# One-pass contraction in the early weighted sums of an attention + SwiGLU kernel, with pair 0's preparation and the weight conversions planned anew

## The chip, the cores and the metric

The kernel runs on one core of a Trainium2 chip. The metric is the device time of one execution in microseconds (us), the median of several runs. The core has five instruction streams that concern us: PE (TensorE, matmuls), DVE (VectorE), ACT (ScalarE), POOL (GpSimd) and SP (SyncE, which here only issues DMAs). They run side by side and wait for each other through semaphores.

## The reference, cut to what matters

```python
q, k, v: (8, 12, 448, 64)          # batch, heads, sequence, head_dim, float32
q_n = q / sqrt(mean(q*q, -1) + 1e-6) * g_q          # the same for k with g_k
attn = softmax(q_n @ k_n.T / 8)                     # over the 448 keys
x = (attn @ v), heads side by side: (3584, 768)
g, val = x @ w_gate, x @ w_val                      # (768, 1536) each, stored as float64
out = (g * sigmoid(g) * val) @ w_out                # (1536, 768), stored as float64
```

## The kernel before, in words

**Tiling.** Two heads of one batch make a pair; there are 48 pairs, six for each batch. A pair holds its two heads one above the other in the 128 partitions (64 of head_dim each). Two batches make one of four blocks of the feed-forward part (896 tokens). The feed-forward part computes its products by a fast 3x3 scheme with 15 products in place of 18: sums of blocks of the operands (function `sides` for the tokens, `convert` for the weights) are multiplied, and the results are added up in PSUM and SBUF ("reads").

**Stages.** First come the 12 early pairs (`m < EARLY`, both batches of block 0), alone on PE. Then block 0's up products (120 products of two matmuls each, gate products into `mm` banks and value products into `at` banks, line 1416), then its down products (line 1594) with pairs 12 to 23 between them, then block 1, and so on. Only the early stage and block 0 also carry the conversion of the weights: 24 pieces are loaded (L1215, L1217), turned from float64 to float32 on ACT (L1225, L1229) and DVE (L1246, L1252, L1258), combined on POOL (L1279, L1282: 15 results) and stored to DRAM (L1307), from where the up and down products load them (L1371).

**A pair.** `attention(m)` does: load q, k (L748 for the early pairs) and v (L771, L774); square q and k on ACT (L784); add up each head's squares on DVE (L804); the inverse root, estimated on ACT (L698, L699) and improved on DVE (L704 to L706); scale on POOL (L843); eight transposes on PE (L869, `turn`); copy the turned k to SBUF on DVE (L875) and the turned q on ACT with the gains `gg` (L877). Then scores in four pieces of keys j = 3, 0, 1, 2 (L927; j = 3 is half a piece), with an exp on ACT after each (L942); the weighted sums (L1003, `weighted`) over the four pieces; the sums of the exps (L1034, `total`); the inverse of these (DVE L1070 and L1072, ACT L1085 `exchange`, DVE L1089 `spread`); and the division (L1098).

**The weighted sums before.** For each key piece of 128 rows, four matmuls work on quarters of the array: 64 keys by 64 values each, 448 queries long. So the upper and the lower 64 keys land in two banks (`at` 0 and 1), which ACT copies out (L1092, `copy_sums`) and DVE joins (L1095, `join`).

**What sets the order.** The order of instructions on each engine is written by a planner, the class `Order`: each piece is added with an engine, a duration, a due time (`when`), what it comes `after`, and the buffers that it takes and uses; `run` then imitates the engines with those durations and emits each piece where its imitation starts it. `LEAD`, `PAIR`, `FIRST`, `MORE`, `block_start` and `pair_time` set the due times, `rank` a lead over others, `SWITCH` a price for a change of mode. On the chip each engine follows its own emitted order, and waits only for semaphores. Buffers matter too: two pairs of `st` banks for scores and for turned q and k, two `at` banks, seven `e` tiles, and nine places for conversions (two in `xs`, `hs`, `spare`, three in `gt`, `es`, and the pairs' `work`), which the stages of the kernel share.

Of the kernel before, what the change touches and what calls it, by code (L numbers as in the profile page):

```python
# [364 lines left out]
class Order:  # L365
# [10 lines left out]
    SWITCH = dict(PE=0.1, ACT=1.3)  # L376
    HOP, ISSUE, LANDING, PLACES = 0.15, 0.54, 2.0, 8

# [52 lines left out]
    def run(self, lookahead=400):  # L431
# [3 lines left out]
        while any(left.values()):  # L435
            best = None
            for engine, pieces in left.items():
                choice = None
                last = self.last.get(engine, dict(group=None))
                for piece in pieces[:lookahead]:  # L440
# [10 lines left out]
                    if choice is None or at < choice[0] - 0.4:  # L451
                        choice = (at, piece)
# [40 lines left out]
def fast(  # L493
# [62 lines left out]
    R = S // NJ  # L556

# [26 lines left out]
    def take(name, key, shape):  # L584
        if name in ("e", "ea"):
            at = order.turn[name] % BUFS[name]
            tiles[name, key] = es[:, at] if at < BUFS["e"] else more_es[:, at - BUFS["e"]]
            return tiles[name, key]
        if name in OFTEN:
# [21 lines left out]
        pool = psum if name in ("st", "at") else sbuf  # L611
# [31 lines left out]
    banks = [psum.tile([P, TB], F32, name=f"mm{i}", bufs=1) for i in range(2)]  # L643
    many = const.tile([P, C], F32, name="many")
# [10 lines left out]
    LEAD, PAIR = 10.6, 8.97  # L655
# [4 lines left out]
    MORE = 6.4  # L660
# [29 lines left out]
    def inverse_root(m, sums, of, when, rank=0.0, tiny=0.0):  # L690
# [10 lines left out]
        def improve():  # L701
# [4 lines left out]
            times(rr, ss, 1.5, rr, op0=ALU.add, op1=ALU.mult)  # L706

# [15 lines left out]
    def attention(m):  # L723
# [52 lines left out]
        load_v = add("SP", 2.4, ready - 16.0, load_values, takes=[("v", m)], moves=VALUE_MOVES, early=25.0)  # L776

        def square(x):
# [5 lines left out]
            nc.scalar.activation(tiles["t", m][:, x], of, AF.Square)  # L784
            if m == 0 and x == 0:
                for _ in range(3):
                    nc.tensor.matmul(banks[0], ident[0:R], of, start=True, stop=True)

        squares = []
        for x in range(2):  # L790
            squares.append(
                add(
                    "ACT", 0.63 if natural else 0.58, ready - 18.0, lambda x=x: square(x),
# [4 lines left out]


# [21 lines left out]
        def both():  # L821
# [5 lines left out]
        sums = add(  # L827
            "DVE", 1.45 if natural else 1.08, ready - 17.0, summed, after=squares, uses=[("t", m)], takes=[("ss", m)]
# [10 lines left out]
        def scale(x):  # L839
            if natural:  # L840
                split = dict(h=2, j=NJ, d=D)
                rr = tiles["rr", m][:, ts(x, 2 * NJ)].rearrange("p (h j one) -> p h j one", h=2, one=1)
                nc.gpsimd.tensor_tensor(  # L843
# [13 lines left out]
                "POOL", 0.98, ready - 9.0, lambda x=x: scale(x), after=[rr], port=True,  # L857
# [6 lines left out]
        def turn(x):  # L864
# [3 lines left out]
            for j in range(NJ):  # L868
                nc.tensor.transpose(turned[:, ts(j, R)], tiles["t", m][:, x, ts(j, P)], ident[0:R, 0:R])  # L869

# [19 lines left out]
        if natural:  # L890
            of_turned = ("st", (m, "turned"))
            for x in (1, 0):
                qt = add(
                    "PE", 0.4, ready - 6.0, lambda x=x: turn(x), after=[scaled[1 - x], qt],
                    uses=[("t", m)] + [of_turned] * (1 - x), takes=[of_turned] * x, mode="full",
                )
                kt = kt or qt
# [7 lines left out]
            )  # L905
        kt = kt or add(
# [89 lines left out]
        def weighted(j):  # L996
            for x in range(2):
                if j == 0:
                    take("at", (m, x), [P, TB])
                rows = ds(D * x, D)  # L1000
                queries = ds(0, S) if j < NJ - 1 else ts(x, Q)
                for h in range(2):
                    nc.tensor.matmul(  # L1003
                        tiles["at", (m, x)][ds(D * h, D), queries],
                        tiles["v", m][rows, j, h],
                        tiles["e", (m, j)][rows, h],
# [37 lines left out]
        last = None  # L1044
        for j in range(NJ):
# [6 lines left out]
                group=("c", m + 1), mode="quarters",  # L1052
            )
        clusters[m, "weighted"] = last
        den = ("st", (m, "d"))
        all_sums = clusters[m, "total"] = add(
            "PE", 1.5 if early else 0.38, when + (0.05 if early else 0.3), total,
            after=[last, *adds] + ([bank_read[0]] if of_bank else []),
            uses=[weights_of(j) for j in range(NJ)] if early else [("sums", m)],
            takes=[] if of_bank else [den], group=("c", m + 1), mode="strips",  # L1060
        )
        if m == EARLY - 1:
            last_exp[0] = all_sums
# [11 lines left out]
        def inverse():  # L1075
            if not early:
                return tiles["at", (m, 0)][:, 0:S]
            return bank[:, 0:S] if of_bank else spread_st[0][:, 1, 0:S]

# [708 lines left out]
```

## Time and profile before

| what | us |
|---|---|
| median of 3 runs | 1462.22 (1462.16 to 1463.76) |
| the profiled execution's own time | 1464.89 |
| its span in the profile | 1463.1 |
| PE busy | 1429.7 (98%) |
| DVE busy | 881.6 (60%) |
| ACT busy | 605.4 (41%) |
| POOL busy | 398.3 (27%) |
| first score matmul of pair 0 (L927) | 14.85 |
| first sum matmul of pairs 0, 1, 2 (L1034) | 34.76, 43.66, 52.52 |
| first up product of block 0 (L1416) | 134.66 |
| last up product of block 0 starts | 313.65 |
| first score matmul of pair 12 | 318.02 |

The profile is of one execution, and times in it count from the span's start. "Busy" counts an engine's instructions; a stretch of PE can be busy at half clock. In the timeline, a line is a run of like instructions: start, length, engine, source line, what is written from what, the shape, the count, and in brackets how long the engine had been idle before it and what ended that. Most matmuls leave two records (those of L869 one), so "x16" of L927 is eight matmuls.

### The profile page before, as it was taken

The numbers are of one execution on the slowest core, as the hardware profiler recorded it, in microseconds if no ns is written. First come the engines' busy times: TensorE is split into PE (matmuls) and PEld (weight loads), VectorE is DVE, ScalarE is ACT, GpSimd is POOL, SyncE is SP. The second block draws the span as 40 slices with busy tenths as digits, with TensorE's granted clock in tenths as the row PEclk, the third lists the DMA queues.
The fourth block names the chain that finished last, engine by engine and source line by source line (L and its number), as shares of the span: only waits on it lengthen the run. The fifth ranks groups of instructions, "written<-read, shape, count | busy, mean of one in ns | idle before, by whom it ended". The sixth has DMA issues, their size and how long they took to land.

```text
span 1463.1 us, 19387 instructions
## 1 busy us (share of the span) xinstructions
PE 1429.7 (98%) x6726; PEld 685.1 (47%) x6726; DVE 881.6 (60%) x1493; ACT 605.4 (41%) x1222; POOL 398.3 (27%) x471
## 2 busy tenths in 40 slices
PE   6998999999999999999999999999999999999997
PEld 2443555544444455544444455554444445555553
DVE  3889977867866444446767632365676643432533
ACT  5885543457563221355654222254656322122100
POOL 3555786535343000012434200012344300000000
PEclk9999999999999999999999999999999999999999
DMA  7667998954454523443553532453454452322235
GB/s 209 185 189 254 337 313 285 297 139 92 102 103 96 133 72 109 110 101 87 118 116 71 118 99 75 117 118 84 103 116 87 96 134 73 102 78 81 78 99 108
DMA packets 410415, 193.28 MB, mean 132 GB/s; under 512 B 280004, under 2 KB 390852, under 8 KB 410308
## 3 DMA queue, kind: packets, MB, share of 16 engines
q1 hardware_dynamic: 399040, 190.57, 48.3%
q10 hardware_dynamic: 11140, 1.38, 0.7%
q8 instruction: 55, 0.90, 0.3%
q14 instruction: 52, 0.43, 0.1%
q0 software_dynamic: 128, 0.00, 0.0%
HBM read 157.29 MB, written 34.60 MB: 131 GB/s over the span
## 4 chain that ended last, share of the span: by engine, by line
PE 90%; DVE 3%; ACT 2%; DMA 2%; issue 1%; SPq 1%; POOL 0%; DVEq 0%; ACTq 0%; POOLq 0%
PE mm L1416 25%; PE at L1416 25%; PE mm L1594 23%; PE st L927 8%; PE at L1003 7%; PE st L1034 1%; ACT es L942 1%; PE mm L1034 1%; DMA out_dram<-spare 1%; DMA work<-in_k_dram 1%; DVE xs L1132 0%; PE st L869 0%; DMA xs<-in_moe_w_gate_dram 0%; DVE spare L1642 0%; DVE mm L1252 0%
## 5 line engine op out<-in xcount | busy, mean ns | idle before, releaser
L1416 PE MATMUL mm<-xs,ws 128*128 128x448 f32 x960 | 400.3, 540 | 0.0
L1416 PE MATMUL at<-xs,ws 128*128 128x448 f32 x960 | 400.2, 539 | 0.0
L1416 PEld LDWEIGHTS at<-xs,ws 128*128 128x128 f32 x960 | 182.3, 190 | 178.9 <-issue 174.7
L1416 PEld LDWEIGHTS mm<-xs,ws 128*128 128x128 f32 x960 | 182.4, 190 | 178.8 <-issue 174.1
L850 POOL TENSOR_TENSOR work<-work,rr 128x448 f32<-128x448 f32 x72 | 67.0, 952 | 468.6 <-DVE rr L706 381.9
L1594 PE MATMUL mm<-gt,ws 128*128 128x448 f32 x448 | 176.1, 544 | 0.0
L927 PE MATMUL st<-work 64*64 64x448 f32 (+1 forms) x1536 | 157.6, 517 | 13.7 <-ACT es L942 6.2
L942 ACT ACTIVATE es<-st 128x896 f32<-128x896 f32 x129 | 114.1, 913 | 110.5 <-PE at L1003 94.1
L1594 PE MATMUL mm<-hs,ws 128*128 128x448 f32 x384 | 151.8, 546 | 0.0
L1354 DVE TENSOR_TENSOR gt<-gt,mm 128x448 f32<-128x448 f32 x64 | 39.8, 621 | 184.3 <-PE mm L1416 182.8
L947 POOL TENSOR_TENSOR sums<-es 128x896 f32<-128x896 f32 x36 | 77.5, 2153 | 184.2 <-PE st L1034 111.2
L1594 PEld LDWEIGHTS mm<-gt,ws 128*128 128x128 f32 x448 | 83.5, 190 | 83.2 <-issue 81.7
L1490 ACT ACTIVATE st<-gt 128x448 f32<-128x448 f32 x96 | 52.6, 547 | 164.9 <-DVE gt L1358 82.0
L1352 ACT COPY gt<-mm 128x448 f32<-128x448 f32 x80 | 42.5, 531 | 167.4 <-PE mm L1416 167.2
L1003 PE MATMUL at<-es,v 64*64 64x448 f32 x1032 | 109.0, 538 | 2.6 <-DVE xs L1095 2.6
L1594 PEld LDWEIGHTS mm<-hs,ws 128*128 128x128 f32 x384 | 71.5, 191 | 72.9 <-issue 71.8
L927 PEld LDWEIGHTS st<-work 64*64 64x64 f32 x1536 | 51.9, 136 | 86.8 <-issue 40.1
L1352 ACT COPY v<-at 128x448 f32<-128x448 f32 x96 | 50.9, 530 | 76.4 <-PE at L1416 74.0
L947 POOL TENSOR_TENSOR sums<-sums,es 128x896 f32<-128x896 f32 x36 | 75.2, 2089 | 2.8
L1003 PEld LDWEIGHTS at<-es,v 64*64 64x64 f32 x1032 | 40.1, 134 | 61.5 <-issue 54.5
L784 ACT ACTIVATE work<-work 128x448 f32<-128x448 f32 (+1 forms) x96 | 55.2, 587 | 25.8 <-DMA work<-in_q_dram 17.1
L1354 DVE TENSOR_TENSOR v<-v,at 128x448 f32<-128x448 f32 x64 | 39.7, 621 | 41.2 <-PE at L1416 41.2
(160 smaller groups left out, 1566.9 us busy)
## 6 DMA issues: line engine op xcount, KB each, us to landing
ws<-up_sides SPq DMA_DIRECT2D x32, 1024.0 KB, 5.6
ws<-down_sides SPq DMA_DIRECT2D x16, 1024.0 KB, 5.7
ws<-down_sides SPq DMA_DIRECT2D x28, 512.0 KB, 4.6
ws<-up_sides SPq DMA_DIRECT2D x16, 768.0 KB, 4.8
out_dram<-spare SPq DMA_DIRECT2D x168, 56.0 KB, 2.1
v<-in_v_dram SPq DMA_DIRECT2D x96, 96.0 KB, 2.6
ws<-up_sides SPq DMA_DIRECT2D x32, 256.0 KB, 5.9
ws<-up_sides SPq DMA_DIRECT2D x16, 512.0 KB, 5.8
```

Of the source, the lines that this page charges most:

```text
L784: nc.scalar.activation(tiles["t", m][:, x], of, AF.Square)
L850: nc.gpsimd.tensor_tensor(out=tiles["t", m][:, x], in0=tiles["qk", (m, x)], in1=rr.to_broadcast([P, NC, C]), op=ALU.mult,)
L927: nc.tensor.matmul(st[ds(D * x, D), h, 0:n], tiles["KT", m][rows, ds(P * j + D * of_keys, D)], tiles["QT", m][rows, ds(Q * of_queries, n)] ...
L942: nc.scalar.activation(e, tiles["st", (m, j)][:, :, 0 : S * width(j) // P], AF.Exp)
L947: nc.gpsimd.tensor_tensor(out=to, in0=tiles["e", (m, 0)] if j == 1 else to, in1=e, op=ALU.add)
L1003: nc.tensor.matmul(tiles["at", (m, x)][ds(D * h, D), queries], tiles["v", m][rows, j, h], tiles["e", (m, j)][rows, h], start=j == 0, stop= ...
L1034: nc.tensor.matmul(to[ds(D * h + C * x, C)], halves[:, x] if half else many[:, 0:C], term[:, h, 0:Q] if half else term[:, h, ts(x, Q)], st ...
L1352: nc.scalar.copy(to, ps)
L1354: nc.vector.tensor_tensor(out=to, in0=old, in1=ps, op=ALU.add)
L1416: nc.tensor.matmul(ps(), w[:, which, c, at], xs[:, SLOT[x], c], start=fresh and c == 0, stop=c == NC2 - 1, skip_group_check=True,)
L1490: nc.scalar.activation(take(*act, [P, 2, TB])[:, 0, 0:S], to, AF.Silu)
L1594: nc.tensor.matmul(banks[s][:, 0:S], w[:, s, g, at], where[x][:, g], start=fresh and g == 0, stop=g == NG - 1, skip_group_check=True,)
```

## The change

- **Weighted sums of the early pairs.** Key pieces 0 to 2 are contracted in one go: 128 keys by 64 values, 224 queries long. The two banks now hold the two halves of the queries instead of the two halves of the keys, so the copy and the join fall away, and `divide` reads both banks straight from PSUM. The inverse is spread into the pair's place in `xs` instead of a bank. The half piece (j = 3) stays as it was. The two `at` banks become one tile `at_banks`.
- **Order of sums.** `total` comes before `weighted`.
- **Pair 0.** Its squares are added up in two halves, its scaling goes from POOL to DVE, its two turns become one piece, and some matmuls of zeros are put on PE from the start (`warm`); `gg` is made on POOL.
- **Pairs 2 and 3** are squared on POOL (`SQUARED`) instead of ACT. Pair 1's sum comes after pair 0's turn.
- **Plan.** Loads of v are due later, the first weight loads ahead of them; the conversions have other due times, places and ranks (`turns`, `starts`, `spans`); some token sums (`sides`) are due 16 us sooner; block 0's first two steps do their gate products before their value products, and the first value products also come after pair 11's weighted sums. No conversion, product or pair is dropped.

```diff
-    SWITCH = dict(PE=0.1, ACT=1.3)
+    SWITCH = dict(PE=0.2, ACT=1.3)
...
+        if name == "at":
+            at = (order.turn[name] - 1) % 2 if key[0] == "up" else key[1]
+            tiles[name, key] = at_banks[:, at]
...
+    at_banks = psum.tile([P, 2, TB], F32, name="at", bufs=1)
...
-    LEAD, PAIR = 10.6, 8.97
+    LEAD, PAIR = 10.4, 8.97
+    HEAD = 2
...
-    MORE = 6.4
+    MORE = 4.4
...
-        load_v = add("SP", 2.4, ready - 16.0, load_values, takes=[("v", m)], moves=VALUE_MOVES, early=25.0)
+        load_v = add(
+            "SP", 2.4, base - 2.0 if early else ready - 16.0, load_values, takes=[("v", m)], moves=VALUE_MOVES,
+            early=4.0 if early else 25.0,
+        )
...
-            nc.scalar.activation(tiles["t", m][:, x], of, AF.Square)
-            if m == 0 and x == 0:
-                for _ in range(3):
-                    nc.tensor.matmul(banks[0], ident[0:R], of, start=True, stop=True)
+            if m in SQUARED:
+                nc.gpsimd.tensor_tensor(out=tiles["t", m][:, x], in0=of, in1=of, op=ALU.mult)
+            else:
+                nc.scalar.activation(tiles["t", m][:, x], of, AF.Square)
+            if m == 1 and x == 1:
+                warm(of[:, 0:S])
...
-                nc.gpsimd.tensor_tensor(
+                engine = nc.gpsimd if m else nc.vector
+                engine.tensor_tensor(
...
-                rows = ds(D * x, D)
-                queries = ds(0, S) if j < NJ - 1 else ts(x, Q)
+                half = j == NJ - 1
+                rows = ds(0, P) if early and not half else ds(D * x, D)
+                queries = ts(x, Q) if half else ds(0, S)
+                of_keys = ts(x, Q) if early and not half else ds(0, Q if half else S)
                 for h in range(2):
                     nc.tensor.matmul(
-                        tiles["at", (m, x)][ds(D * h, D), queries],
+                        tiles["at", (m, x)][ds(D * h, D), ds(0, Q) if early else queries],
                         tiles["v", m][rows, j, h],
-                        tiles["e", (m, j)][rows, h],
+                        tiles["e", (m, j)][rows, h, of_keys],
...
+        last = sum_up(clusters.get((m - 1, "weighted"))) if early else None
...
-            nc.vector.transpose(inverse(), every.to_broadcast([P, 2 * Q // C, C]))
+            to = x if early else tiles["at", (m, 0)][:, 0:S]
+            nc.vector.transpose(to, every.to_broadcast([P, 2 * Q // C, C]))
...
+            if early:
+                to = x.rearrange("p (x q) -> p x q", x=2)
+                nc.vector.tensor_tensor(out=to, in0=to, in1=at_banks[:, :, 0:Q], op=ALU.mult)
+                return
...
-        copied = add(
-            "ACT", 0.53, when + 3.0, copy_sums, after=[last, up_done.get(b // 2 - 1)], uses=at[:1]
-        )
-        joined = add("DVE", 0.62, when + 4.0, join, after=[copied, last], uses=at[1:])
+        copied, joined = None, last
+        if not early:
...
-                    "DVE", 0.62, when,
+                    "DVE", 0.62, soon if soon is not None and i in (6, 8, 1, 10, 13, 9) else when,
...
-        rank = 0.0 if by_bank else 20.0
+        rank = 0.0 if by_bank else 5.0
...
-    turns = [(*XS, HS, SPARE, GT[1], GT[0], HS), (ES, PAIRS, GT[2], SPARE, HS), (ES, HS, PAIRS, SPARE)]
-    starts = [LEAD - 4.0, FIRST - 24.2, FIRST + 78.2]
-    spans = [11.0, 8.2, 9.9]
+    turns = [(XS[0], XS[1], HS, SPARE, GT[1], GT[0], HS, SPARE, GT[1],), (SPARE, PAIRS, HS, GT[2], ES,), (PAIRS, SPARE, ES, HS,)]
+    starts = [LEAD - 3.4, FIRST - 40.1, FIRST + 78.2]
+    spans = [9.9, 8.3, 9.9]
```

## The prediction

> **What bounds the kernel now.** The page's first part says PE, and the chain that ended last agrees:
>
> ```profile
> PE 1429.7 (98%) x6726; PEld 685.1 (47%) x6726; DVE 881.6 (60%) x1493; ACT 605.4 (41%) x1222; POOL 398.3 (27%) x471
> PE 90%; DVE 3%; ACT 2%; DMA 2%; issue 1%; SPq 1%; POOL 0%; DVEq 0%; ACTq 0%; POOLq 0%
> ```
>
> So time can be won only where PE is idle or slow. The busy times by stage (stretch, length, busy of each engine with counts, PE clock, DMA share, GB/s) show where: the stretches are the fill, the regular early pairs, their end, and most of block 0's up products.
>
> ```profile
> 0.00:26.15 26.15, 14.91 (x63) 6.26 (x63) 7.87 (x18) 12.88 (x23) 7.50 (x19) 0.97 0.83 226
> 26.15:98.00 71.85, 70.81 (x845) 33.89 (x846) 56.31 (x116) 62.43 (x118) 41.00 (x63) 0.96 0.64 188
> 98.00:134.70 36.70, 30.73 (x350) 13.31 (x348) 34.65 (x65) 23.15 (x42) 21.52 (x37) 0.95 0.60 202
> 134.70:260.00 125.30, 125.30 (x338) 63.48 (x335) 102.81 (x156) 59.76 (x82) 82.78 (x161) 1.00 0.92 314
> ```
>
> PE is full from 134.70 on; from there to the end, 1328.4 us, it stands idle only some 6 us. The change must earn before 134.7. PE's timeline names the holes:
>
> ```profile
> 14.85 2.52 PE L927 MATMUL st<-work 64*64 64x224 f32 x16 [0.72 <-ACT work L877]
> ...
> 26.15 4.76 PE L927 MATMUL st<-work 64*64 64x448 f32 x24 [3.15 <-ACT es L942]
> ...
> 34.76 1.34 PE L1034 MATMUL mm<-es,many 128*32 128x224 f32 x24
> ...
> 110.09 0.98 PE L927 MATMUL st<-work 64*64 64x448 f32 x8 [1.82 <-DVE work L875]
> ...
> 122.11 0.59 PE L1003 MATMUL at<-es,v 64*64 64x448 f32 x2 [2.62 <-DVE xs L1095]
> ...
> 130.22 0.59 PE L1003 MATMUL at<-gt,v 64*64 64x448 f32 x2 [1.08 <-DVE xs L1095]
> ```
>
> Scores start at 14.85, but pair 0's sums only at 34.76: ACT does a conversion and four squares (20.28 to 24.41) ahead of pair 0's last exps. Later PE waits for DVE (L875, and the join L1095 that frees an `at` bank), which is 94% busy from 98 to 134.7. One hole lies after block 0:
>
> ```profile
> 318.02 2.52 PE L927 MATMUL st<-work 64*64 64x224 f32 x16 [2.70 <-ACT work L884]
> ```
>
> **What the Trainium skill says.** "TensorE: Matmul & The Clock Gate", section "What's actually happening": after an idle window of about 3.4 us PE runs at half clock. The trace agrees: after 3.15 us idle, the 12 matmuls at 26.15 take 4.76 us, where three such groups cost 2.25 elsewhere; the granted clock of 25 to 30 is 0.50. "TensorEngine Tiling (Array Packing)", section "Key Properties": a change of tiling mode drains PE, and different tiles run in parallel. Both show: the scores after the strips of L1034 take 1.29 us against 0.38 + 0.75, so 0.16 a change; and 16 strip matmuls 224 long take 1.65 us together, four at a time. The same clock page, section "Architectural detail: the array is 16× 32×32, not 1× 128×128": ACT and DVE take their queue strictly in order. The fill shows it, and I use it below. "DMA: Bandwidth & Descriptors", section "Anatomy of one DMA", has a fixed 2 us; here the stores of L1307 land in 3.7 to 10.4, median 5.9, and that is used.
>
> **Part by part.**
>
> *The contraction.* A key piece costs 0.75 us now (four quarters of 448 at once). Four matmuls of 224 in two column halves, two at once, are 2 x 0.375 = 0.75: nothing gained. If the halves don't overlap it is 1.5, the upper bound; the strips of L1034 share rows and differ in columns as these do, so I take 0.75. The order strips, halves, quarters has one change of mode more a pair; with another where a turn splits them I take 0.34 a pair (0 to 0.5). A pair's PE work is then scores 2.63 + sums 1.65 + weighted 2.63 + turns 0.93 + changes 0.5 = 8.35, against 8.45 measured between pairs 1 and 8 ((103.23 - 43.66) / 7 = 8.51, waits included).
>
> *Copy and join.* ACT loses 12 x 0.53 = 6.4 us, DVE 12 x 0.61 = 7.3. Neither is a gain as such; it counts where that engine paces PE. Both `at` banks are now held until the division, which needs the sums, inverse (0.65), exchange on ACT (0.82) and spread (0.67). Sums first hides these 2.1 us behind the 2.63 of weighted sums. Queued behind the division's wait on DVE are conversions and the next pair's drains; PE's next weighted sums come at least 1.65 later, against 0.2 + 0.62 for the division.
>
> *The fill.* I followed the changed order of instructions with the old durations. q and k of pairs 0 and 1 land as before (3.8 to 7.7). Pair 0's inverse root starts on ACT at about 7.2, ahead of the last square, and its scaling takes 2 x 0.69 on DVE instead of 2.04 on POOL: turned at 10.3, first scores at 11.3 instead of 14.85. Now ACT has one conversion copy (1.28; its weights, issued fifth, have about 2.1 MB before them at 0.3 MB/us and land near 10), then the four exps of pair 0 in a row: sums of pair 0 at 16. Scores of pair 1 from 17.7; pair 2 hangs on q and k (landing near 16 behind 4 MB), POOL squares 2 x 1.04, and scaling behind the squares of pair 3 on POOL (landing near 22): its turn ends at 25.3, where pair 1's sums start. Then ACT's copies for two conversions (4 x 1.28) and pair 4's squares, waiting for DMA near 29, hold the exps: pair 2's sums at 39.5. Before it was 52.52, with 2.63 of weighted sums already done that now follow. So the fill gains 52.5 - 39.5 - 2.7 = about 10. Error: plus or minus 4, mainly the DMA landings.
>
> *From pair 2's sums to block 0.* Ten sums 16.5, ten weighted 26.3, eight scores 21.0, seven turns 6.5, changes 10 x 0.5: 75.3 us of PE. Before, with nine weighted: 71.1, and it took 134.66 - 52.52 = 82.1: 11 us lost. DVE: adding up its rows in the emitted order, the stretch from pair 7's division to pair 11's (102.1 to 140.2) held 37.7 us of work in 38.2: DVE was the bound. In the changed order the same stretch holds 29.3: the four joins 2.4, and 6 us of conversions that now stand earlier. Over the whole early stage DVE falls from 110.5 to 102.5 us, and from pair 2's sums to pair 11's division it has 73 us, under PE's 75.3 but close. So some waits remain: I take 0.45 a pair, 4.5 (0 to 11). ACT has about 63. Block 0 starts at 39.5 + 75.3 + 4.5 = 119.3; say 120, 14.7 earlier.
>
> *Does it stay won?* Up products are 180.6 us of PE with no hole. Eight conversions are emitted before the first read in both orders, and the last ends at the 58th read in both: relative to block 0 the weights come as before. DMA is at 0.92 there, with the same bytes. The reordered first products cost nothing: gates 8 and 6 take 3.0 us, over the 2.9 until pair 11's division. What is late next is pair 12. Its scores now stand ten products (15 us) before the end of the up products. On DVE, behind the 62nd read, stand the transposes of pairs 12 and 13 and sums that need the last conversion's store; reads 63 onward are queued behind them, and their banks hold PE. The scaling on POOL is behind the last conversion, which ends near 164 us after block 0's start (298.6 in the trace): pair 12 is turned near 169.5, where PE wants it at 165.6. That is 4 us of hole and about 1 of half clock, in place of 2.7 and 1.4 now; more changes of ACT's table stand there too (1.28 each). I take +1.5 (-3 to +6). SP: pair 12's loads are issued ahead of the last stores, eight DMAs of 0.5, in that estimate.
>
> *Sum.* Span 1463.1 - 14.7 + 1.5 = 1449.9. The profiled execution took 1464.89, 1.8 over its span, and the median is 2.7 below it: 1449.9 + 1.8 - 2.7 = 1449.0. The walk knows no waits that it doesn't see, so I shade it by 1: 1450.
>
> **Rivals.**
>
> 1. *Half of it: DVE stays the pace.* With 73 us of DVE against 75 of PE, strictly in order, waits of a pair add up. If they stay as before (11 instead of 4.5) and the fill gains 7 instead of 10, it is 1450 + 6.5 + 3 = 1459. For: DVE's 94%. Against: its densest pairs fall from 12.4 and 10.6 to 10.8 and 8.9, each followed by a light one.
> 2. *More: the waits vanish.* PE runs the early pairs at 8.35 without waits and pair 12 comes in time: 1450 - 4.5 - 3 = 1442. Against: ACT and DVE both stand over 80% there.
> 3. *Slower: column halves don't overlap.* Three pieces x 12 pairs x 0.75 = 27 us more of PE, all on the path: 1450 + 27 = 1477; it turns slower than before from 0.34 us a piece on (12 / 36). Against: the strips. For: no row of the trace has 128x64 tiles.
> 4. *No gain.* The early gain is given back where block 0 waits for weights or pair 12: 1462. For: DMA's 0.92. Against: no hole there now.
>
> **Chances.** Forecast (1445 to 1455) 50%; rival 1 (1455 to 1459.3) 23%; rival 2 (below 1445) 15%; rival 4 (within 0.2%, 1459.3 to 1465.1) 6%; rival 3 or otherwise slower 6%. A measurement tells about 0.2% from no change. Range for 8 in 10: 1443 to 1459. Faster 0.88, same 0.06, slower 0.06.
>
> **What would show it.** Right: first scores near 11.3, sums of pairs 0 and 2 near 16 and 39.5, first up product near 120; weighted pieces of 0.75; PE waits of the early pairs under 5 us in all after pair 2; a hole of 3 to 6 us on ACT's or DVE's turn at pair 12. Wrong: a first up product later than 127 (DVE busy near 95% ahead of it: rival 1), pieces near 1.5 (rival 3), or holes in the up products that name a weight load (rival 4).

## The result and the profile after

The changed kernel takes 1457.64 us (median of 7, 1456.57 to 1460.45), before beside it 1462.32 (7 runs): ratio 0.9966, 95% interval 0.9955 to 0.9976. Faster, as forecast, and inside the range; but the gain is 4.7 us, and the forecast was 12.3.

The page of the changed kernel, busy times and the chain that ended last:

```profile
PE 1424.7 (98%) x6736; PEld 689.5 (47%) x6736; DVE 880.6 (61%) x1484; ACT 601.8 (41%) x1210; POOL 401.0 (28%) x476
PE 90%; DMA 4%; ACT 2%; DVE 2%; SPq 1%; issue 1%; POOL 0%; DVEq 0%; ACTq 0%; POOLq 0%
```

PE is the bound as before. Its stages (stretch, length, busy of PE, PEld, DVE, ACT and POOL with counts, PE clock, DMA share, GB/s), cut where block 0 now starts:

```profile
0.00:26.15 26.15, 19.36 (x137) 9.22 (x138) 10.94 (x27) 14.44 (x26) 9.71 (x24) 0.93 0.84 234
26.15:98.00 71.85, 67.10 (x793) 35.33 (x793) 58.78 (x121) 60.38 (x114) 48.42 (x72) 1.00 0.66 200
98.00:125.14 27.14, 26.36 (x337) 14.15 (x337) 25.39 (x45) 14.45 (x26) 16.70 (x28) 1.00 0.76 237
125.14:260.00 134.86, 133.23 (x357) 66.81 (x354) 108.15 (x164) 62.11 (x86) 82.96 (x163) 1.00 0.91 311
```

The third stage, which starts at the same clock time in both, shrank from 36.7 to 27.1 us. DVE is still 94% busy in it, but PE is at 97% where it was at 84%: DVE no longer makes it wait. Of the 9.5 us by which block 0 starts earlier, 5.9 are less idle time of PE (18.2 to 12.3 us before block 0) and 2.6 are clock: by the traces' clock records, PE stood at half clock for 10.2 us before block 0 in before (6.83 from 24.4, 3.41 from 123.4) and for 3.4 in the changed kernel (from 11.4), which cost 4.2 and 1.6 us of its busy time. PE's timeline at the places shown of before:

```profile
15.20 1.36 PE L965 MATMUL st<-work 64*64 64x224 f32 x16 [0.67 <-ACT work L913]
20.24 1.34 PE L1074 MATMUL mm<-es,many 128*32 128x224 f32 x24
44.10 1.34 PE L1074 MATMUL mm<-es,many 128*32 128x224 f32 x24
45.75 2.49 PE L1043 MATMUL at<-es,v 128*64 128x224 f32 x24
53.86 0.98 PE L965 MATMUL st<-work 64*64 64x448 f32 x8 [0.47 <-ACT work L913]
295.98 1.36 PE L965 MATMUL st<-work 64*64 64x224 f32 x16 [2.56 <-ACT work L920]
```

The fourth line is three key pieces in column halves: 0.8 us each, change of mode included. Rival 3 (halves don't overlap) is refuted. The first line is no earlier than before (14.85), and ACT's timeline says why (the first line is before's, the others are the changed kernel's):

```profile
6.81 0.63 ACT L784 ACTIVATE work<-work 112x512 f32<-112x512 f32 x1 [1.68 <-DMA work<-in_q_dram]
...
8.12 0.63 ACT L801 ACTIVATE work<-work 112x512 f32<-112x512 f32 x1 [3.06 <-DMA work<-in_q_dram]
8.66 0.29 ACT L706 ACTIVATE rr<-ss,little 112x16 f32<-112x16 f32 x1
9.49 0.63 ACT L801 ACTIVATE work<-work 112x512 f32<-112x512 f32 x1 [0.29 <-DMA work<-in_k_dram]
```

The square of pair 1's q waits for its load until 8.12 (6.81 before), and pair 0's inverse root (L706) stands behind it, though its sums were ready at 5.8. On SP, five weight loads now follow the four loads of q and k, where before had loads of v (2.69):

```profile
2.70 1.48 SPq L1266 DMA_DIRECT2D xs<-in_moe_w_gate_dram  x3
4.23 1.94 SPq L1268 DMA_DIRECT2D xs<-in_moe_w_gate_dram  x2
```

Where the forecast and the trace part, in us of the profiled executions:

| point | before | forecast | after |
|---|---|---|---|
| first scores | 14.85 | 11.3 | 15.20 |
| sums of pair 0 | 34.76 | 16 | 20.24 |
| sums of pair 2 | 52.52 | 39.5 | 44.10 |
| first up product | 134.66 | 120 | 125.14 |
| block 2's first up product | 837.0 | | 827.9 |
| last matmul ends | 1455.7 | | 1446.5 |
| span | 1463.1 | 1449.9 | 1455.4 |
| median | 1462.32 | 1450 | 1457.64 |

The 7.6 us between 1450 and 1457.64 add up: block 0 starts 5.1 later than forecast (4.6 of it at pair 2's sums); from there to block 2 it is 702.8 us against 702.4 before, where I had put 1.5 more, so 1.1 comes back; from the last matmul to the span's end it is 8.9 instead of 7.4, 1.5 more. And the median lies 0.4 above the profiled execution, where I had subtracted 2.7 and added 1: another 2.1.

### The profile page after: what moved, and what is told of

Read it like the earlier page. It is cut to its first block, busy times and chain, and to the rows that moved or that the text cites. A ratio compares the mean times of both kernels' runs of the same rounds, so it can differ in the third digit from the quotient of the medians.

```text
span 1455.4 us, 19339 instructions
## 1 busy us (share of the span) xinstructions
PE 1424.7 (98%) x6736; PEld 689.5 (47%) x6736; DVE 880.6 (61%) x1484; ACT 601.8 (41%) x1210; POOL 401.0 (28%) x476
## 4 chain that ended last, share of the span: by engine, by line
PE 90%; DMA 4%; ACT 2%; DVE 2%; SPq 1%; issue 1%; POOL 0%; DVEq 0%; ACTq 0%; POOLq 0%
PE at L1467 24%; PE mm L1467 24%; PE mm L1650 24%; PE at L1043 8%; PE st L965 7%; PE st L1074 1%; ACT es L980 1%; DMA xs<-in_moe_w_gate_dram 1%; DMA out_dram<-spare 1%; PE mm L1074 1%; SPq L764 0%; DMA work<-in_k_dram 0%; PE st L903 0%; DMA hs<-in_moe_w_val_dram 0%; DMA work<-in_q_dram 0%
## 5 line engine op out<-in xcount | busy, mean ns | idle before, releaser
L965 PE MATMUL st<-work 64*64 64x448 f32 (+1 forms) x1536 | 151.0, 500 | 11.8 <-ACT work L913 4.6
L1403 ACT COPY gt<-mm 128x448 f32<-128x448 f32 x80 | 42.6, 532 | 165.3 <-PE mm L1467 165.1
L1043 PE MATMUL at<-es,v 64*64 64x448 f32 (+1 forms) x1032 | 106.0, 507 | 0.0
L1403 ACT COPY v<-at 128x448 f32<-128x448 f32 x96 | 51.0, 531 | 80.0 <-PE at L1467 80.0
L1043 PEld LDWEIGHTS at<-es,v 64*64 64x64 f32 (+1 forms) x1032 | 44.1, 134 | 56.2 <-issue 48.6
L1547 DVE SCALAR_TENSOR_TENSOR gt<-st,v 128x448 f32<-128x448 f32 x96 | 59.7, 623 | 7.7 <-DVE v L1407 0.5
```

The costliest lines, as they stand in the source:

```text
L965: nc.tensor.matmul(st[ds(D * x, D), h, 0:n], tiles["KT", m][rows, ds(P * j + D * of_keys, D)], tiles["QT", m][rows, ds(Q * of_queries, n)] ...
L1043: nc.tensor.matmul(tiles["at", (m, x)][ds(D * h, D), ds(0, Q) if early else queries], tiles["v", m][rows, j, h], tiles["e", (m, j)][rows, ...
L1403: nc.scalar.copy(to, ps)
L1547: nc.vector.scalar_tensor_tensor(to, tiles[act][:, 0, 0:S], 1.0 / SCALE, tiles[ready], op0=ALU.mult, op1=ALU.mult,)
```

## The experiments

Every kernel is the changed one with the edit named, unless said otherwise; "up" is the start of the first up product, "end" the end of the last matmul, "tail" from there to the span's end, all of the profiled execution (for delay_pe, "up" is the first product after the added matmuls). Two profiled executions of one kernel differ by 2.2 us at up and 0.5 at end (before), by 1.1 and 1.4 (the changed kernel), so smaller differences in these columns say nothing. Some expectations count block 2 from the semaphore in front of its first product's weights, 3.3 us ahead of the product (824.6, so 699.5 from up in the changed kernel). Ratios are to the runs of before on the same chip (medians 1463.6 to 1464.7), with 95% intervals.

| kernel | median | ratio | up | end | tail |
|---|---|---|---|---|---|
| before_again | 1463.45 | 0.9998 (0.9990-1.0007) | 136.9 | 1456.2 | 7.4 |
| after_again | 1458.97 | 0.9968 (0.9956-0.9980) | 126.3 | 1448.0 | 9.0 |
| root_first | 1458.92 | 0.9962 (0.9949-0.9976) | 125.0 | 1448.7 | 9.0 |
| root_no_of | 1459.12 | 0.9974 (0.9964-0.9985) | 126.3 | 1448.5 | 9.1 |
| v_first | 1456.58 | 0.9951 (0.9938-0.9965) | 125.2 | 1447.4 | 9.0 |
| pool_order | 1456.54 | 0.9957 (0.9944-0.9971) | 125.3 | 1448.1 | 8.8 |
| fill_all | 1457.09 | 0.9957 (0.9943-0.9970) | 124.9 | 1447.6 | 7.4 |
| contr_alone | 1487.48 | 1.0169 (1.0155-1.0183) | 157.6 | 1478.2 | 7.4 |
| contr_sums | 1466.56 | 1.0020 (1.0012-1.0027) | 136.3 | 1456.6 | 7.4 |
| rows | 1458.29 | 0.9964 (0.9950-0.9977) | 134.8 | 1449.5 | 7.4 |
| old_plan | 1465.22 | 1.0015 (1.0007-1.0023) | 123.8 | 1450.7 | 10.2 |
| late_12 | 1463.62 | 0.9996 (0.9988-1.0005) | 125.1 | 1449.0 | 10.2 |
| pairs_early | 1464.07 | 1.0003 (0.9994-1.0011) | 124.2 | 1453.1 | 7.4 |
| ws_ahead | 1457.35 | 0.9957 (0.9944-0.9971) | 125.4 | 1447.2 | 7.6 |
| delay_pe | 1468.15 | 1.0024 (1.0016-1.0032) | 136.7 | 1458.0 | 8.9 |
| best | 1453.78 | 0.9934 (0.9920-0.9947) | 121.7 | 1443.9 | 7.4 |
| best_rows | 1457.33 | 0.9957 (0.9943-0.9970) | 127.8 | 1446.0 | 7.4 |

### How much of the gain is real: before_again, after_again

No edit. Before:

> The kernel before, unchanged, once more. Theory C (the profiled execution of before held a stretch of half clock that its other executions don't have: 12 matmuls at 26.15 took 4.76 us, 2.25 elsewhere): ratio 1.000, a profiled span near 1460.5 instead of 1463.1, with that group near 2.3 to 3 us and a mean granted clock of about 0.996, so that about 2.5 us of the 7.7 us between the two profiled spans are no gain of the change. Rival: the 2.5 us lie outside the fill (stores at the end, what lies around the span): the span or the group stays as it was.

Theory C fell: the second profile has the half-clock group too (4.75 us after 3.14 idle) and a span of 1463.7. After:

> The changed kernel once more, unchanged, beside before on the same chip as the variants. If the small gain of the first comparison (4.7 us, against 7.7 between the two profiled spans) lay in the few executions of before that it had (7, median 1462.3, against 1463.6 to 1464.0 in the three comparisons since), the ratio is now 0.995 to 0.9965, 5 to 7 us; if the gain really is 4.7, it is 0.9965 to 0.9975. Markers in the trace as in the first profile: first up product 125, last matmul near 1446.5, 8.9 us from there to the end.

Ratio 0.9968: the gain is 4.7 to 5.1 us. The profiled executions overstate it (7.7 and 6.7 between spans): those of before lie at the slow end of their runs (1461.5 to 1466.0 for before_again), those of the changed kernel in the faster half. The 2.7 that I took off was a difference between one execution and three; it belongs to before and was no property to carry over.

### The fill: root_first, root_no_of, v_first, pool_order, fill_all

```diff
-        first = order.add("ACT", 0.48, ...)
+        first = clusters["root", m] = order.add("ACT", 0.48, ...)
...
-                    after=[loaded[x], *squares], ...
+                    after=[loaded[x], *squares, clusters.get(("root", 0)) if m == 1 else None], ...
```

> The changed kernel with one order changed: ACT does pair 0's inverse root (ready to start at 5.8 us) ahead of the square of pair 1's q, which waits for its load until 8.1. Theory A (this place in ACT's queue costs the first scores 3 us): scaling starts at 7.0 instead of 9.86. Rival B (the warm-up matmuls in PE's queue hold the turn; the one on pair 1's k waits for that load, 9.5 us): the turn moves only from 12.05 to about 11, first scores to 14 instead of 15.2. Both: the time changes by 1 us at most. Theory D (what pair 0 gains is lost again by pair 2, whose scaling is behind the squares of pair 3 on POOL, and these wait for a load until 25.9): first up product within 1 us of 125.1.

Of root_first, ACT and then PE:

```profile
5.88 0.31 ACT L706 ACTIVATE rr<-ss,little 112x16 f32<-112x16 f32 x1 [0.82 <-DVE ss L820]
7.83 0.63 ACT L801 ACTIVATE work<-work 112x512 f32<-112x512 f32 x1 [1.40 <-DMA work<-in_q_dram]
```

```profile
9.26 1.02 PE L1741 MATMUL mm<-work,more 112*128 112x448 f32 x2 [0.68 <-DMA work<-in_k_dram]
10.12 0.93 PE L903 MATMUL st<-ident,work 112*128 112x112 f32 x8
12.49 1.36 PE L965 MATMUL st<-work 64*64 64x224 f32 x16 [1.05 <-ACT work L913]
```

The place in ACT's queue cost 2.7 us at the first scores (A), and the warm-up matmul on pair 1's k did wait for its load (B, first line). Without that matmul:

```diff
-                warm(of[:, 0:S])
+                pass
```

> As root_first, and without the warm-up matmul on pair 1's k, which computes nothing that is used. If A and B both hold: scaling at 7.0, turn at about 8.3, first scores at about 12 (bound by the product of the gains, ready at 10.6) instead of 15.2, pair 0's sums 1.5 to 3 us earlier than 20.24. If only A: first scores at 14; if neither: 15. Theory D then says: pair 2's sums stay within 1 us of 44.1 and the first up product within 1 us of 125.1, time within 1 us. Its rival, that pair 0's delay passes straight through to block 0: first up product near 122, time 3 us less.

First scores at 10.70, then PE waits 2.77 us for exps that stand behind a weight conversion on ACT, and goes on at half clock (the next 8 matmuls take 2.91 us instead of 1.79). The other cause of the late start is on SP:

```diff
 (load_values, pair 0)
+            if m == 0: held.pop()()
 (convert)
-        loaded = add("SP", 2.5, when - 12.0, load, ...)
+        loaded = add("SP", 2.5, when - 12.0, (lambda: held.append(load)) if key == ("up", 0) else load, ...)
```

> The changed kernel with one swap in SP's queue: the four loads of pair 0's v ahead of the five loads of the first weight block, as before had v there. Theory E (the weight loads, issued right behind pair 1's q and k, take the transfer engines from these): the square of pair 1's q starts near 6.8 to 7 instead of 8.12, that of its k near 7.7 to 8.3 instead of 9.49, pair 0's inverse root 1 to 1.3 us earlier, first scores near 14.1. Rival: the landing is set by something else (the order in which packets of the four loads are served): square at 8.1 as now. The first conversion's copy may then wait for its weights, issued 3.7 us later: up to 1 us there. Time within 1 us either way if theory D holds.

ACT of v_first:

```profile
6.62 0.63 ACT L801 ACTIVATE work<-work 112x512 f32<-112x512 f32 x1 [1.48 <-DMA work<-in_q_dram]
7.16 0.29 ACT L706 ACTIVATE rr<-ss,little 112x16 f32<-112x16 f32 x1
```

Theory E holds: 1.5 us earlier with v in place of weights behind it; scores at 12.59. Yet up stays at 125 to 126 in all three: in root_first pair 2's sums start at 44.12, as without it. So theory D was asked:

```diff
+        scaled = clusters["scaled", m] = [ ... ]
 (squares of pair 3, on POOL)
+        after=[..., *(clusters.get(("scaled", 2), []) if m == 3 else [])]
```

> The changed kernel with root_first's order on ACT, and on POOL the squares of pair 3, which wait for their load until 25.9, behind the second scaling of pair 2. Theory D (with pair 0 earlier, pair 2's turn is what PE waits for; it hangs on that queue): pair 2's scaling ends near 26.5 instead of 28.9, its turn moves forward as much, pair 1's sums near 28 and pair 2's near 42.5 instead of 44.1, first up product near 123.5, time 1 to 2 us under the changed kernel. Rival: the next wait takes its place (pair 2's exps on ACT stand behind squares of pair 5, whose load lands near 37): pair 2's sums stay at 44, first up product at 125.

Its rival was right (44.27). With ACT's next entry moved as well:

```diff
 (squares of pair 5, on ACT)
+        after=[..., clusters.get(("exps", 2)) if m == 5 else None]
```

> pool_order, and on ACT the squares of pair 5, which wait for their load until 37, behind the last exps of pair 2. Theory D2 (one queue entry after another holds the fill, and with ACT's freed as well pair 2's sums come as predicted order by order): pair 2's sums near 42.5 instead of 44.1 to 44.3, first up product near 123.5. Rival L (the loads themselves pace the fill: SP issues them one behind the other and they land late, so pair 5 pays what pair 2 wins): first up product within 1 us of 125.1, time within 1 us of the changed kernel.

Pair 2's sums came to 40.24, near the forecast's 39.5, but pair 3's only from 49.84 to 49.26, and up to 124.9, as rival L said. Most of the 3.9 us at pair 2's sums is order: a turn and two score pieces (2.9 us) that stood ahead of them now stand behind. What pair 0 had won (first scores at 11.95) went before that:

```profile
23.60 0.98 PE L965 MATMUL st<-work 64*64 64x448 f32 x8 [1.37 <-ACT gt L980]
...
26.31 3.20 PE L1044 MATMUL at<-es,v 128*64 128x224 f32 x16
```

PE waits for pair 1's exps, and the 8 matmuls at 26.31 run at half clock (3.20 us, 1.73 in the changed kernel). That those exps stand on ACT behind pair 2's inverse root, and this behind sums that wait for a load landing at 18.8 us, is read from the queues. Only with the loads in order too does the fill come forward (best, below).

### The contraction: contr_alone, contr_sums, rows

contr_alone puts the contraction alone into before:

```diff
-                rows = ds(D * x, D)
-                queries = ds(0, S) if j < NJ - 1 else ts(x, Q)
+                half = j == NJ - 1
+                rows = ds(0, P) if early and not half else ds(D * x, D)
...
-        copied = add("ACT", 0.53, ...)
-        joined = add("DVE", 0.62, ...)
+        copied, joined = None, last        # early pairs
```

> The kernel before with the contraction alone: weighted sums of the early pairs over all key rows, queries over the two banks, no copy and no join, spread and division on both banks; its own preparation, its own plan of conversions, weighted sums still ahead of the sums over keys. Theory F (copy and join, 6.4 us of ACT and 7.3 of DVE, pace the early pairs of before, whose ten pairs lost 11 us to waits): pieces of 0.75 us, first sums near 35 as before, first up product 3 to 6 us before 134.7 to 136.9, time 3 to 6 us less. Rival G (the banks, now held until the division, which stands behind the sums on PE, make a wait of the same size; it is the order sums first and the plan of conversions that count): first up product within 1.5 us of before or later, time the same or more.

24 us slower than before. Its waits of PE from 20 to 145 us (line that waited, line waited for, us in total, times, longest):

```profile
PE at L1010 <- DVE xs L1107: 11.4, 8, 3.0
PE st L932 <- ACT es L947: 4.8, 3, 3.1
PE st L932 <- ACT work L882: 4.6, 8, 1.0
```

L1107 is the division. The banks are held until it, and it waits for sums that stand behind the weighted sums on PE. contr_sums adds the order of the changed kernel (`total` ahead of `weighted`):

> contr_alone, and the early pairs' sums over keys ahead of their weighted sums, as in the changed kernel; preparation and plan of conversions still those of before. Theory K (the 24 us that the contraction alone costs come from the banks, which are held until a division that waits for sums queued behind the weighted sums on PE): the waits of weighted sums for the division fall from 11.4 us to under 3, first up product near 130 (126 to 134), time within 6 us of before. If the clock or the tiles were the cause of the 24 us, it stays above 145.

The waits for the division fall to 4.4 us (not under 3), and 21 of the 24 us come back; up comes to 136.3 (not 130):

```profile
PE at L1010 <- DVE xs L1115: 4.4, 3, 2.8
```

K is the cause, the size was off. On the old plan even both together are no gain, but 3 us slower than before. And the changed kernel with the contraction undone:

```diff
-                rows = ds(0, P) if early and not half else ds(D * x, D)
+                rows = ds(D * x, D)
...
-        if not early:
+        if True:                           # copy and join again
```

> The changed kernel with the contraction undone: early weighted sums in two halves of the key rows again, one bank each, copy on ACT and join on DVE again, the inverse spread into the bank of the sums; sums still first, preparation and plan of conversions as changed. Theory F: first scores at 15.2 and pair 0's sums near 20 as in the changed kernel, then the waits of before: from pair 2's sums to the first up product 85 to 88 us instead of 81.0, first up product near 130, time 4 to 6 us more than the changed kernel. Rival G: first up product within 2 us of 125.1, time within 2 us.

Up at 134.8, 9.7 later: F, and more (from pair 2's sums to up it is 87.6 us, in the 85 to 88 of F; of the 9.7, 3.1 are half clock, 4.7 us of busy time lost to it against 1.6). But the end is only 3.0 later (1.5 against after_again), the tail 1.5 shorter, and the ratio is that of the changed kernel. What the contraction wins before block 0, rows wins back in it and, for 1.5 us, in the tail.

### The plan of conversions: old_plan

```diff
+    turns = [(*XS, HS, SPARE, GT[1], GT[0], HS), (ES, PAIRS, GT[2], SPARE, HS), (ES, HS, PAIRS, SPARE)]
+    starts = [LEAD - 4.0, FIRST - 24.2, FIRST + 78.2]
+    spans = [11.0, 8.2, 9.9]
... (ranks 20 and 70, no earlier combinations, MORE = 6.4, as before)
```

> The changed kernel with the conversions planned as before (buffers in turn, starts, spacing, precedence; first combinations not brought forward). Theory H (the new plan moves conversions off DVE ahead of block 0, 6 us of them, and with that shortens the waits of the last early pairs): the stretch from pair 2's sums to the first up product grows from 81.0 to 84 us or more, DVE again over 90% busy from 98 us on, time 3 us or more above the changed kernel. Rival: the early pairs hide it, first up product within 1.5 us of 125.1, and only the scores of pair 12 near 296 move: time within 2 us.

Theory H fell where it was put: up is at 123.8, earlier than with the new plan. But the kernel is 7 us slower ((1.0015 - 0.9967) x 1464), and the end of block 0 shows a part:

```profile
311.17 1.85 PE L965 MATMUL st<-work 64*64 64x224 f32 x16 [3.78 <-ACT work L920]
312.96 4.43 PE L1650 MATMUL mm<-hs,ws 128*128 128x448 f32 x8
```

Pair 12's scores wait 3.78 us, and what follows is at half clock (4.43 for 3.27).

### The end of block 0: late_12, pairs_early, ws_ahead, delay_pe

From up to block 2 the changed kernel takes 702.8 us, rows 696.7. PE's waits there, changed kernel (first six lines up to 500 us):

```profile
PE st L965 <- ACT work L920: 2.6, 1, 2.6
PE at L1467 <- DVE v L1409: 1.0, 1, 1.0
PE at L1467 <- DVE v L1407: 0.9, 1, 0.9
PE at L1467 <- ACT v L1403: 0.6, 1, 0.6
PE st L1074 <- issue: 0.4, 1, 0.4
PE st L965 <- PE st L965: 0.2, 1, 0.2
...
PE st L965 <- ACT es L980: 1.3, 5, 0.4
PE at L1467 <- DVE v L1405: 0.8, 1, 0.8
PE st L1074 <- ACT more L980: 0.4, 1, 0.4
```

and rows (three lines up to 500 us):

```profile
PE st L965 <- DVE gt L1544: 0.6, 1, 0.6
PE at L1464 <- ACT v L1400: 0.6, 1, 0.6
PE at L1464 <- DVE v L1406: 0.4, 1, 0.4
...
PE st L965 <- ACT es L980: 0.6, 2, 0.4
PE st L1074 <- ACT more L980: 0.4, 1, 0.4
```

8.2 us against 2.6: more than five of the six are waits, the largest pair 12's. Moved three products back:

```diff
 (scores of pair 12)
+                after=[..., clusters.get(("up", 0, NG - 1, 11, 0)) if m == EARLY else None],
```

> The changed kernel with pair 12's first scores three up products (4.5 us) later in PE's order, at the end of block 0. Theory I (of the 9.7 us by which the contraction brings block 0 forward, measured against the kernel without it, 6 are lost again between the first up product and block 2, because pair 12's preparation is tied to the last conversions and not to PE's start): the hole of 2.6 us in front of these scores goes, first up product to block 2's first goes from 699.5 to about 697, last matmul near 1444 instead of 1446.5, time 2 to 3 us less. Rival J (the wait only moves: scores that come later make pair 12's exps, sums on POOL and weighted sums late in the down products): new waits of 2 to 3 us between 315 and 340, last matmul within 1 us of 1446.5.

Theory I fell in this form. The hole went, and another wait, for a load that the hole may have covered, appeared at the same place:

```profile
295.37 2.84 PE L1467 MATMUL mm<-xs,ws 128*128 128x448 f32 x4 [1.99 <-DMA ws<-up_sides]
```

These are the last up weights, whose load stands on SP behind 16 DMAs for pairs 12 and 13 (issued 278.2 to 289.0). The other way to pair 12:

```diff
-    ... (PAIRS, SPARE, ES, HS,)]
+    ... (PAIRS, SPARE, ES, PAIRS, HS, SPARE, ES, HS)]
```

> The changed kernel with one order of buffers changed among the last eight conversions, so that the buffer that pair 12's q and k need is free one conversion earlier; in the plan this puts pair 12's scaling ahead of the last conversion's 7 us on POOL, and its scores two to four up products before the end of block 0. Theory I: no hole in front of pair 12's scores, last conversion stored 2 to 4 us later with nobody waiting for it, last matmul near 1443 to 1444, time 2 to 4 us less. Rival J: the hole is replaced by waits for the conversions that are now late or by later steps of pair 12: last matmul within 1 us of 1446.5 or later.

Rival J: waits for weights, 1.2 and 4.0 us, and 6.5 us later at the end (5.1 against after_again). With SP's order changed instead:

```diff
 (loads of pairs 13 and later)
+                after=[..., clusters.get(("ws", 0, NG - 1, 10)) if EARLY < m < EARLY + 8 else None],
```

> The changed kernel with one order on SP: the load of the last up weights of block 0 ahead of pair 13's q and k loads (eight DMAs, 5.2 us of issue) instead of behind them; in the plan this also puts pair 12's scores three up products later, as in late_12. Theory M (at the end of block 0 two things are late at the same time, 295 us: pair 12's queries and the last up weights, whose load stands behind 16 DMAs on SP; taking away one alone shows the other, as late_12's wait of 2.0 us for these weights did): neither wait remains, block 0's first to block 2's first up product goes from 699.5 (701.8 in late_12) to 697 or less, last matmul near 1444. Rival J (the lost time comes from pairs 12 and 13's own chain, exps and scores among the first down products): the waits of 1.5 and 0.8 us near 321 to 328 stay or grow, last matmul at 1446.5 to 1449.

Both waits are gone, the idle time from up to block 2 falls to 5.4 us, and it still takes 703.2: PE is busy 3 us longer from up to the end (1314.8 for 1311.8), and the planner's new order splits the scores into smaller groups between the products, with more changes of mode. That these are the 3 us was not isolated. The time is 1.6 us under after_again, 1.4 of it in the tail, and the intervals of the ratios overlap. So the order was kept, and only PE's lead taken away:

```diff
+                for _ in range(13 if (n, g, step, which) == (0, 0, 0, 0) else 0):
+                    nc.tensor.matmul(ps(), w[:, 0, 0, at], xs[:, SLOT[x], 0], start=True, stop=True)
                 for c in range(NC2):
```

> The changed kernel with 13 further matmuls of the up product's form (13 x 0.75 = 9.8 us, their result is overwritten) on PE in front of the first up product, everything else in its order: PE starts block 0 as late as the kernel with the contraction undone, the rest of the machine as early as the changed kernel. Theory N (what block 0 needs at its end, the last weights and pair 12's operands, does not start earlier because PE does, so PE's lead of 9.7 us is mostly idle time there): the idle time between the first up product and block 2 falls from 8 us to 3 to 4, last matmul at 1450 to 1452, 3 to 5 us later than without the 9.8 us of added work. Rival O (PE is the bound, and the kernel without the contraction does better in block 0 only by its other order): last matmul at 1455 to 1457.5, the whole 9.8 us later.

PE of delay_pe, the added work and pair 12's scores:

```profile
126.85 10.04 PE L1467 MATMUL mm<-xs,ws 128*128 128x448 f32 x26
307.24 1.63 PE L965 MATMUL st<-work 64*64 64x224 f32 x16 [2.56 <-ACT work L920]
```

Theory N fell: the hole is the same 2.56 us, moved along by 11, and the end is 10.0 later than in after_again, which also has 3.41 us of half clock after this hole, and 11.4 later than in the first profile, which has none: all of the added work. From up to block 2 it is 702.7 us, as in the changed kernel. PE is the bound through block 0. The hole follows PE because pair 12's steps stand behind the products' reads in the queues of ACT and DVE. What remains for rows is rival O: another order in block 0, with over 5 us less of waits. This is by exclusion; which of its differences does it was not isolated.

### The version that beats both: best, best_rows

best joins the edits of fill_all, v_first and ws_ahead:

> ws_ahead, with the fill's four orders together (pair 0's inverse root ahead of the square of pair 1's q, pair 3's squares behind pair 2's scaling, pair 5's squares behind pair 2's exps, pair 0's v ahead of the first weight block). If both ends add up: first up product at 124, last matmul at 1442 to 1443, time 1452 to 1454, below both kernels. If rivals L and J hold: last matmul at 1446 to 1448, time as the changed kernel's.

PE of best, first scores and sums of pair 2:

```profile
11.57 1.36 PE L965 MATMUL st<-work 64*64 64x224 f32 x16 [1.05 <-ACT work L913]
37.67 1.34 PE L1075 MATMUL mm<-es,many 128*32 128x224 f32 x24
```

1453.78 us, ratio 0.9934 (0.9920 to 0.9947): 10 us under before, 5 under the changed kernel, of which 1.6 are the tail (7.4 for 9.0). Up at 121.7 is 3.7 us before ws_ahead's, and the end 3.3 before: a gain of the fill is kept to the end. No order alone gave more than 0.2 us at up, the four of ACT, POOL and SP together 3.7. The contraction undone in best:

> best with the contraction undone as in rows. If the contraction's 9.7 us are given back in block 0 whatever the fill does (theory N), the time is within 3 us of best (1453.8): last matmul at 1444 to 1447. If best, which takes two waits from the end of block 0, keeps what the contraction wins: 4 to 8 us above best.

Up 6.1 later, end 2.1, median 3.5: between the two expectations. The contraction is worth 2 to 3.5 us here (the intervals of the two ratios overlap), and again most of what it wins before block 0 is lost in it. From up to block 2 best takes 703.3 us, best_rows 700.0.

## Why the prediction was right or wrong, step by step

- *Contraction, 0.75 us a piece:* right. Change of mode and pieces as taken.
- *Copy and join, DVE as the pace:* right in kind. After pair 2's sums block 0 starts within 81.0 us (forecast 79.8 with 4.5 of waits; PE was idle for 3.9); its waits for DVE there are gone, those left are for ACT. That the bank's hold needs "sums first" was right: contr_alone against contr_sums prices it at 21 us.
- *The fill:* this step failed, in its landings: "q and k of pairs 0 and 1 land as before (3.8 to 7.7)" and the inverse root "at about 7.2". With five weight loads behind them in place of v, pair 1's landed at 8.1 and 9.5, and pair 0's root stood behind the first: 4.2 us late at pair 0's sums. My own paragraph on ACT's strict order was not applied to a load that lands late. The later landings were too early by as much: pair 2's q and k, put near 16, landed at 19.5 and 20.3, pair 3's first, put near 22, at 25.8. The 4.6 us at pair 2's sums are not pair 0's delay handed on, since root_first took 2.7 us off pair 0 and left them at 44.12: the next pairs' entries wait for their own loads. v_first and root_first show the two halves at pair 0 (v_first also has pair 2's q at 16.8). With all four orders best has first scores at 11.57 and block 0 at 121.7, so most of the forecast's fill could be had.
- *Does it stay won?* Right in sum. The hole is 2.56 (4 taken), waits for reads on DVE add 2.7, and block 0 to block 2 takes 0.4 us more than before (1.5 taken). The half clock behind the hole (1 taken) came in after_again and not in the first profile. The eight DMAs on SP that I counted were sixteen, and the load behind them was of weights, covered only by pair 12's hole, as late_12 suggests.
- *Reordered first products cost nothing:* 0.6 us of wait (L1403) did come of it or of the copy it waits for.
- *Sum:* the 2.7 between one profiled execution and a median was subtracted from a sum that it did not belong to: 2.1 of the 7.6.
- *Not seen:* the tail, 1.5. It goes with the build: 7.4 to 7.6, 8.8 to 9.1 or 10.2 us among these kernels, within 0.2 in the two that were profiled twice. The stores have all landed by 4.2 us after the last matmul in both; what follows are packets of the instruction queue, one of them 2 us later in the changed kernel than in before. But best has such a late packet too, at 8.7, and a tail of 7.4, so the packets alone don't explain it, and the cause stays open.
- *Rival 1* (1459, half of it) named the right size for another reason: DVE was not the pace.

## What to carry to other kernels

When a change puts new loads beside old ones, price the landing of the old ones again, and then every entry that stands behind the waiting one in its engine's queue; a start gained there counts only when all the queues of the next pairs move with it. Value the parts of a change by undoing each: here the contraction was worth 0 to 3.5 us, and the plan of conversions beside it 7, more than the whole gain (pair 0's preparation and the squares on POOL were not undone by themselves). Compare more than one profile: half clock and the tail moved these ends by as much as the orders did. And when a removed hole gives nothing, look at what it covered.

## What the runs showed of the hardware that was not expected

The same idle time can cost a clock change or not, even in one kernel. In the changed kernel's first profile, PE is idle for 2.56 us in front of pair 12's scores, their first 8 matmuls take 1.36 us (line 295.98 above), and the granted clock of the next 3 us is 1.00. After the same hole in after_again and pool_order:

```profile
297.10 2.05 PE L965 MATMUL st<-work 64*64 64x224 f32 x16 [2.56 <-ACT work L920]
...
296.09 2.52 PE L965 MATMUL st<-work 64*64 64x224 f32 x16 [2.56 <-ACT work L920]
```

The clock is at 0.50 for 3.41 us, from 0.5 us after the hole in after_again, from 0.2 before its end in pool_order. Up to the last matmul, every low-clock record of these traces is at 0.50 and lasts 3.41 or 6.83 us, so one of the short ones costs PE up to 1.7 us (an estimate: half of 3.41). late_12 has one after 1.99 us of idle, fill_all one from 25.9 after holes of only 1.37 and 0.40. The Trainium skill, "TensorE: Matmul & The Clock Gate", section "What's actually happening", speaks of an idle window of about 3.4 us that runs free, so that the effect varies from run to run. The traces agree on the varying and on the length; they show half clock after shorter holes than 3.4 us, the 3.15 that the prediction reads as agreement among them, and there the measurement decides. Whether this is a part of the up to 4.5 us by which executions of one kernel differ (1461.48 to 1465.96 in before_again) was not tried.
